# Attention and a two-layer network on one core: the second layer of the first two blocks as seven half-size products, with sums of its weights by VectorE

## The chip, the core and the metric

The kernel runs on one core of a Trainium2 chip. The core has TensorE (PE: matrix products, reading SBUF and writing PSUM), VectorE (DVE), ScalarE (ACT), GpSimd (POOL) and SyncE (SP), each with an instruction stream of its own that runs strictly in order. Engines wait for each other by semaphores. Transfers are issued from a queue of SP, ACT or POOL and moved by 16 shared DMA engines. The metric is the device time of one execution in microseconds (us); lower is better. "PE" is TensorE's row of matmuls and "PEld" its row of weight loads in the profile.

## The reference

```python
# q, k, v: (8, 8, 576, 64) float32; w_in: (512, 2048); w_out: (2048, 512); tau = 0.02
scores = (q @ k.transpose(0, 1, 3, 2)) / sqrt(64)
thresh = scores.max(-1, keepdims=True) - tau
scores = where(scores >= thresh, scores, -1e9)
attn = exp(scores - scores.max(-1, keepdims=True))
attn = attn / (attn.sum(-1, keepdims=True) + 1e-9)
x = (attn @ v).transpose(0, 2, 1, 3).reshape(4608, 512)
h = x @ w_in
out = (h * (1 / (1 + exp(-1.702 * h)))) @ w_out
```

Everything is float32: 64 heads of attention with a threshold one tau below the row's maximum, then a two-layer network over 4608 rows.

## The kernel before

**Units.** Attention is worked in 32 pairs of heads, n = 0 to 31; four pairs make the 576 rows of one batch. The network is worked in 18 blocks of 256 rows. A block can start when the pairs that cover its rows are placed: blocks 0 and 1 need pairs 0 to 3, blocks 2 and 3 need up to pair 7, blocks 4 and 5 up to pair 11.

**A pair.** PE makes transposed scores (L590), ACT copies them out of PSUM (`keep`, L607), VectorE takes maxima (`in_groups`, L613), ACT and VectorE join them across partitions, and the row of maxima is spread over all partitions. VectorE subtracts it (`sub`, L687), ACT masks (L694) and exponentiates (L698), VectorE sums (L613 again), PE multiplies with v (`values`, L709), and VectorE multiplies by the reciprocals of the sums and places the pair into x (`place_x`, L813). From pair 7 on PE interleaves the values of one pair with the scores of the next, tile by tile, because both use the same score tiles.

**Rows.** For pairs 1 and 3 to 6 the row of maxima goes to DRAM (`row_out`, L663) and comes back broadcast (`row_in`, L672); some tiles get it by an accumulating transfer (`add_row`, L678). For pairs 4 to 31 the reciprocals of the sums make the same trip (`sums_out` L778, `sums_in` L785). Each was two transfers, one for each half of the partitions or each head. Pairs below 8 issue them from POOL's queue, the others from SP's.

**The network.** The weights come in 32 pieces (16 of w_in, 16 of w_out) that ACT and VectorE round in a few instructions each (L520, L524, L538, L545). Blocks 0 and 1 run together and plainly: layer one by `mm1_ahead` and `mm1_0` (L876, L887) with 16 chunks of 128 hidden units, `tanh` on ACT and `gelu_0` on VectorE into `g0`, then layer two by `mm2` (L856): 4 row tiles x 16 chunks, 64 matmuls of 512 columns, copied out by ACT (`half`, L863) and stored. From block 2 on both layers use the seven-product scheme on 2x2 quarters: layer one in `product1`, `product0`, `product4` (L955, L1097), layer two in `product` (L1397), in the order P1, P2, P6, P7, P4, P5, P3, each product being 8 matmuls of 256 columns. Its right operands are quarters of w_out and four sums of them (t1, t2, t4 and t3, which is made in place); its left operands are quarters of the activations and their sums on VectorE (`s_sums`, `s_minus`, `s_last`, L1013 to L1024). `read` (L1412, L1419) adds each product into the output quarters. The four sums of w_out are made by `t_minus` (ACT, L997, two sign copies each) and `t_plus` (an accumulating transfer of 1 MB on POOL's queue, L1001), the sums of w_in in the same way by `w_copy` (L922) and `w_plus` (L926). The last four blocks use the scheme twice over (L1248, L1357).

**The order.** Nothing is scheduled at run time. `task` describes each piece of work (engine, estimated cost, rank, predecessors, pools taken and given), and `run_in_order` plays the tasks through a list scheduler with these estimates; whenever an engine is free, the ready task of lowest rank is emitted. FIRST (-9) goes ahead of everything; attention has its pair's number plus a bias by function from the tables EARLY, SECOND and LATER; weights have W_RANK and CV, loads L_RANK; network products have LAST (1000). So on PE attention goes ahead of the network whenever it is ready. A pair n may not start scores before task 16 x (n - LEAD) of the network. Pools bound what is ahead: 3 double banks of PSUM for attention (psA), 2 banks for the network (psM), 6 buffers of x (xT).

**Fillers.** `stay_warm` emits WARM small matmuls on ones at the lowest rank of all, for the time before the network starts (L1463).

## Time and profile before

| | us |
|---|---|
| median of 3 runs | 1224.17 (1223.91 to 1225.14) |
| profiled execution | 1225.39 |
| its span | 1223.6 |
| PE busy | 1212.8 (99% of the span) |
| VectorE busy | 1059.3 (87%) |
| ACT busy | 803.1 (66%) |
| POOL busy | 71.0 (6%) |

The profile is of one execution. Its page gives busy times by engine, the span in 40 slices, the chain of work that ended last, and the costliest groups. Other views of the same trace are quoted too: a table of stretches (columns: the stretch, its length, then busy time and count of PE, PEld, DVE, ACT and POOL, TensorE's granted clock as a share of full speed, the busy share of the DMA engines, GB/s), a timeline (start, length, engine, line, operation, output and inputs, count; in square brackets the idle time before it and what ended it), groups by line and shape (count | busy us, mean ns | idle us before, what ended it), and the instructions of one tile (duration min/median/max in ns, first and last start). A float32 matmul leaves two records that overlap.

### The profile page before, as it was taken

The page shows a single profiled execution, that of the slowest core. Times are in us where ns is not written, and L with a number is a line of the kernel's source. Part 1 is how long each engine was busy: PE and PEld are TensorE (multiplying, and loading weights), DVE is VectorE, ACT ScalarE, POOL GpSimd, SP SyncE. Part 2 cuts the span into 40 slices and gives each one's busy share as a digit, 9 for nine tenths or more (in the row PEclk, how much of TensorE's full clock was granted, in tenths as well). Part 3 has the DMA queues.
Part 4 walks back from the last instruction along what each step waited for, and adds up shares of the span by engine and source line. Part 5 has one row for each costly group of instructions (what it writes and reads, how often), then busy time and mean ns, then how long its engine had stood idle before and what let it go on. Part 6 is the DMA issues. An engine that isn't in the chain of part 4 may idle for free.

```text
span 1223.6 us, 26039 instructions
## 1 busy us (share of the span) xinstructions
PE 1212.8 (99%) x10592; PEld 987.0 (81%) x10592; DVE 1059.3 (87%) x1649; ACT 803.1 (66%) x1203; POOL 71.0 (6%) x115
## 2 busy tenths in 40 slices
...
GB/s 203 252 108 199 196 146 190 209 100 58 101 49 110 49 116 56 75 77 126 101 66 103 71 128 76 65 65 128 91 50 67 101 125 50 129 130 141 141 134 103
DMA packets 202232, 137.12 MB, mean 112 GB/s; under 512 B 146880, under 2 KB 164416, under 8 KB 201984
## 3 DMA queue, kind: packets, MB, share of 16 engines
q1 hardware_dynamic: 189712, 110.21, 33.5%
...
q8 instruction: 83, 1.36, 0.5%
q10 hardware_dynamic: 688, 0.30, 0.1%
q14 instruction: 37, 0.30, 0.1%
HBM read 103.28 MB, written 23.75 MB: 104 GB/s over the span
## 4 chain that ended last, share of the span: by engine, by line
PE 92%; ACT 4%; DMA 2%; DVE 1%; issue 0%; SPq 0%; POOL 0%; POOLq 0%
PE ops L1397 24%; PE pv L709 10%; PE ps L590 10%; PE hps L955 7%; PE hps L1097 7%; PE ps L955 5%; PE ps L1097 5%; PE ops L856 5%; PE hps L887 4%; PE ops L1357 4%; PE hps L1248 4%; PE ps L1357 3%; PE ps L1248 3%; ACT arena L694 1%; ACT arena L698 1%; ACT arena L607 1%
## 5 line engine op out<-in xcount | busy, mean ns | idle before, releaser
L613 DVE TRANSPOSE_TENSOR_REDUCE part<-arena 128x36 f32<-128x1152 f32 (+1 forms) x300 | 363.8, 1239 | 65.9 <-ACT arena L607 49.0
L607 ACT COPY arena<-ps 128x576 f32<-128x576 f32 x288 | 170.5, 644 | 96.8 <-PE ps L590 96.8
L694 ACT ACTIVATE arena<-arena 128x1152 f32<-128x1152 f32 (+1 forms) x160 | 165.1, 1060 | 67.7 <-DVE arena L687 67.5
L687 DVE TENSOR_TENSOR arena<-arena 128x1152 f32<-128x1152 f32 (+1 forms) x150 | 180.9, 1240 | 3.4 <-DMA arena<-row 2.8
L698 ACT ACTIVATE arena<-arena,shift 128x1152 f32<-128x1152 f32 (+1 forms) x160 | 180.5, 1154 | 1.5
L590 PE MATMUL ps<-arena 64*64 64x288 f32 x2304 | 171.4, 408 | 3.4 <-ACT arena L607 3.1
L1397 PE MATMUL ops<-w_out,arena 128*128 128x256 f32 x768 | 174.4, 381 | 0.0
L1397 PEld LDWEIGHTS ops<-w_out,arena 128*128 128x128 f32 x768 | 144.3, 190 | 24.9 <-issue 5.3
L709 PE MATMUL pv<-arena 64*64 64x288 f32 x2176 | 158.5, 405 | 0.0
L590 PEld LDWEIGHTS ps<-arena 64*64 64x64 f32 x2304 | 82.2, 132 | 64.1 <-ACT arena L607 25.3
L709 PEld LDWEIGHTS pv<-arena 64*64 64x64 f32 x2176 | 82.2, 133 | 52.2 <-issue 9.1
L1397 PE MATMUL ops<-arena 128*128 128x256 f32 x528 | 118.1, 379 | 0.0
L1397 PEld LDWEIGHTS ops<-arena 128*128 128x128 f32 x528 | 100.2, 190 | 14.0 <-issue 0.4
L1262 ACT COPY arena<-hps 128x512 f32<-128x512 f32 x44 | 25.7, 584 | 58.4 <-PE hps L1248 58.3
...
L856 PE MATMUL ops<-w_out,arena 128*128 128x512 f32 x128 | 55.9, 595 | 0.0
...
L887 PE MATMUL hps<-xT,w_in 128*128 128x256 f32 x232 | 50.8, 380 | 0.0
L887 PEld LDWEIGHTS hps<-xT,w_in 128*128 128x128 f32 x232 | 43.9, 190 | 6.8 <-issue 0.4
L856 PEld LDWEIGHTS ops<-w_out,arena 128*128 128x128 f32 x128 | 24.1, 190 | 30.1 <-issue 29.5
L955 PEld LDWEIGHTS hps<-xT,w_in 128*128 128x128 f32 x384 | 44.2, 192 | 1.1 <-issue 0.9
L955 PE MATMUL hps<-xT,w_in 128*128 128x128 f32 x384 | 44.9, 275 | 0.0
...
## 6 DMA issues: line engine op xcount, KB each, us to landing
arena<-in_v_dram SPq DMA_DIRECT2D x128, 144.0 KB
...
arena<-in_k_dram SPq DMA_DIRECT2D x112, 72.0 KB
arena<-in_q_dram SPq DMA_DIRECT2D x112, 72.0 KB
...
```

The costliest lines, as they stand in the source:

```text
L590: nc.tensor.matmul(ps[ts(c, KT), h, 0:SH], lhsT=mats[n, 1][ts(h, D), ts(j, KT)], rhs=mats[n, 0][ts(h, D), ts(c, SH)], start=True, stop=True,)
L607: nc.scalar.copy(out=sT[n, t][:, u], in_=pss.pop((n, j))[:, :, 0:SH])
L613: nc.vector.tensor_reduce(out=stats[n, op][:, t * 2 * QB : min(2 * t + 2, NK) * QB], in_=sT[n, t].rearrange("p u h (g d) -> p (u h g) d", ...
L687: engine.tensor_tensor(out=s, in0=s, in1=mbs[n].unsqueeze(1).to_broadcast(list(s.shape)), op=ALU.add if n in BY_DMA else ALU.subtract,)
L694: nc.scalar.activation(out=s, in_=s, func=AF.Prelu, alpha=STEEP)
L698: nc.scalar.activation(out=s, in_=s, func=AF.Exp, scale=SCALE, bias=shift)
L709: nc.tensor.matmul(o[c][ts(h, D), 0:SH], lhsT=left(j, h)[ts(c, KT)], rhs=sT[n, t][ts(c, KT), u, h, :], start=(j == 0), stop=(j == NK - 1),)
L856: nc.tensor.matmul(acc[i], lhsT=g0[:, j, ts(i, P)], rhs=w_out[:, j, :], start=(j == 0), stop=(j == NFC - 1),)
L887: nc.tensor.matmul(hidden[j][:, ts(i, BLK)], lhsT=w_in[:, c, ts(j, P)], rhs=xTs[i][:, c, :], start=(c == 0), stop=(c == NDC - 1), skip_gro ...
L955: nc.tensor.matmul(o[:, ts(j, HT)], lhsT=left[:, c, ts(4 * y + j, P)], rhs=right[:, c, :], start=(x in (P1, P2, P5) and j + c == 0), stop= ...
L1097: nc.tensor.matmul(o[:, ts(j, BLK)], lhsT=left[:, c, ts(j, P)], rhs=right[:, c, :], start=(x in (P1, P2, P5) and j + c == 0), stop=(j + c ...
L1397: nc.tensor.matmul(banks[blk][k][:, ts(o, HM)], lhsT=left[:, j, :], rhs=right[:, j, :], start=(j == 0), stop=(j == HF - 1),)
```

## The change

The second layer of blocks 0 and 1 no longer uses `mm2`. It goes through the seven products of the later blocks, block 0 first, then block 1 (MIXED = 1), 15 tasks each, on the quarters of `g0`. Extra room is found in place: block 0's sums go to the tile that held the tanh values (`th`, kept until P5), to the quarter a11 after P1 has read it (`s_second`), and to a12; block 1's go to block 0's quarters after block 0 is done.

The sums of w_out that these two blocks need are made by `t_whole`, whole subtractions on VectorE, in the order t1, t2, t3, t4_0, as soon as all of w_out is rounded. t4 has a seat of its own for these blocks (t4_0, in the area of score tiles, free once pair 5 is placed); the t4 of the later blocks is made after block 1 in the old way, on ACT and POOL. The last sum of w_in uses the same area and now waits for the end of block 1.

Rows: `row_out`, `row_in` and `sums_in` are one transfer each; `sums_out` still is two, with another layout in DRAM. LEAD is 8 instead of 6. `stay_warm` uses 128 columns and both halves of the partitions, 40 times. The planner's estimates for rows change, and all tables of ranks are replaced.

```diff
     EARLY = {
-        "add_row": 53.65,
...
+        "add_row": 61.4,
...
     SECOND = {
...
     LATER = {
...
     CV = {
...
     def row_out(n):
-        rows[n] = dram.tile([2, S], FP32, name="row", tag="row", bufs=2)
-        for c in range(2):
-            row_queue(n).dma_start(
-                out=rows[n][c : c + 1].rearrange("o (g i) -> (o g) i", i=32),
-                in_=flat[1][ds(c * KT, QB)],
-            )
+        r = dram.tile([P, 32], FP32, name="row", tag="row", bufs=2)
+        row_queue(n).dma_start(out=r, in_=flat[1])
+        rows[n] = r.rearrange("(c g) i -> c (g i)", c=2)[:, 0:S]
     def row_in(n):
...
         row = rows[n]
-        for c in range(2):
-            row_queue(n).dma_start(out=mb[ts(c, KT)], in_=row[c : c + 1].to_broadcast([KT, S]))
+        row_queue(n).dma_start(
+            out=mb,
+            in_=row.unsqueeze(1).to_broadcast([2, KT, S]),
+        )
         mbs[n] = mb
...
             row_queue(n).dma_start(
-                out=rcs[n][c].rearrange("h (g i) -> (h g) i", i=32), in_=flat_s[1][ds(c * KT, QB)]
+                out=rcs[n][:, c].rearrange("h (g i) -> h g i", i=32), in_=flat_s[1][ds(c * KT, QB)]
             )
...
         rc, row = seat(rc_pool(n)), rcs.pop(n)
-        for h in range(2):
-            row_queue(n).dma_start(
-                out=rc[ts(h, D)].rearrange("p (c s) -> p c s", c=2),
-                in_=row[:, h].unsqueeze(0).to_broadcast([D, 2, SH]),
-            )
+        row_queue(n).dma_start(
+            out=rc, in_=row.rearrange("h c s -> h (c s)").unsqueeze(1).to_broadcast([2, D, S])
+        )
         rcs[n] = rc
...
-    g0 = arena[:, ds(2 * HF * HM, 2 * NFC * BLK)].rearrange("p (j t) -> p j t", t=2 * BLK)
     PLAIN = 2
...
     t3 = qb[0][1]
-    T_SUMS = [(t1, t3, qb[0][0]), (t2, qb[1][1], t1), (t4, qb[1][0], t2), (t3, qb[1][1], t3)]
+    g0 = arena[:, ds(2 * HF * HM, 2 * NFC * BLK)].rearrange("p (j t) -> p j t", t=2 * BLK)
+    MIXED = 1
+    qas0 = [
+        [[g0[:, ts(f, HF), ds(x * BLK + h * HT, HT)] for f in range(2)] for h in range(2)]
+        for x in range(2)
+    ]
+    t4_0 = arena2[:, ds(room["s_m1"][0][0] + 2 * HF * HM, HF * HM)].rearrange("p (j m) -> p j m", m=HM)
+    s_0 = [g0[:, HF:NFC, ts(x, HT)] for x in range(2)]
+
+    T_SUMS = [
+        (t1, t3, qb[0][0]), (t2, qb[1][1], t1), (t4_0, qb[1][0], t2), (t3, qb[1][1], t3),
+        (t4, qb[1][0], t2),
+    ]
+
+    def left_sums(blk):
+        if blk == 0:
+            return places["th"].rearrange("p (j t) -> p j t", t=HT), qas0[0][0][0], qas0[0][0][1]
+        return (s_0 if blk == MIXED else sg) + [None]
     def t_minus(x, k):
...
         nc.scalar.activation(out=o, in_=b, func=AF.Copy, scale=-1.0)
+    def t_whole(x, k):
+        o, a, b = (y[:, ts(k, HF // 2), :] for y in T_SUMS[x])
+        nc.vector.tensor_tensor(out=o, in0=a, in1=b, op=ALU.subtract)
+
     def t_plus(x):
...
     def quarters(blk):
+        if blk <= MIXED:
+            return qas0[blk]
         if blk < TAIL:
...
         qa = quarters(blk)
-        a11, a21, a22, u1, u2 = (y[:, ts(k, 4), :] for y in (qa[0][0], qa[1][0], qa[1][1], s1, s2))
+        a11, a21, a22, u1, u2 = (
+            y[:, ts(k, 4), :] for y in (qa[0][0], qa[1][0], qa[1][1], *left_sums(blk)[0:2])
+        )
         nc.vector.tensor_tensor(out=u1, in0=a21, in1=a22, op=ALU.add)
+        if blk == 0:
+            return
         nc.vector.tensor_tensor(out=u2, in0=u1, in1=a11, op=ALU.subtract)
...
         nc.vector.tensor_tensor(out=a21, in0=a11, in1=a21, op=ALU.subtract)
+    def s_second(k):
+        u1, a11 = (y[:, ts(k, 4), :] for y in left_sums(0)[0:2])
+        nc.vector.tensor_tensor(out=a11, in0=u1, in1=a11, op=ALU.subtract)
+
     def s_last(blk, k):
-        a12, u = (y[:, ts(k, 4), :] for y in (quarters(blk)[0][1], s2))
-        nc.vector.tensor_tensor(out=u, in0=a12, in1=u, op=ALU.subtract)
+        a12, u = (y[:, ts(k, 4), :] for y in (quarters(blk)[0][1], left_sums(blk)[1]))
+        nc.vector.tensor_tensor(out=u if blk else a12, in0=a12, in1=u, op=ALU.subtract)
     P1, P2, P6, P7, P4, P5, P3 = range(7)
...
         left, right, k, o = PRODUCTS[x]
+        if blk <= MIXED and x in (P6, P5, P3):
+            left = left_sums(blk)[{P5: 0, P6: 1, P3: 1 if blk else 2}[x]]
+        if blk <= MIXED and x == P4:
+            right = t4_0
         if isinstance(left, tuple):
...
         d = psM.tile([P, BANK], FP32, name="up", tag="mo")
-        for _ in range(2):
-            nc.tensor.matmul(d[0:D, 0:D], lhsT=ones[0:KT], rhs=ones[0:KT], start=True, stop=True)
+        for r in range(2):
+            nc.tensor.matmul(
+                d[ts(r, KT), 0:P], lhsT=ones[ts(r, KT)], rhs=eye[ts(r, KT)], start=True, stop=True
+            )
     def tau_terms():
...
     SUMS_BY_DMA = range(4, NP)
-    LEAD = 6
+    LEAD = 8
     ROWS_BY_POOL = range(8)
...
     T_RANK = FIRST
-    W_RANK = (76.72, 196.12, 138.01, 508.95, -9.25, -19.99)
+    W_RANK = (31.97, 148.79, 230.02, 650.9, -20.74, 160.11)
     W_TIME = 1.8
-    WARM = 44
+    WARM = 40
     ROUND_BY_ACT = range(0)
...
     early_mm1, held_sums = [], []
+
+    late_seat = []
     def first_blocks():
...
             gelus[j] = task("DVE", 0.59, FIRST, gelu_0, j, after=[a],
-                give=("psM", "io") + (("xT",) if j == NFC - 1 else ()),
+                give=("psM", "io"),
             )
         plain1[:] = ffn[-1:]
-        for i in range(PLAIN * BLK // P):
-            for p in range(NFC // 2):
-                after = ffn[-1:] + [gelus[2 * p], gelus[2 * p + 1]]
-                after += ready_w[n_in + 2 * p : n_in + 2 * p + 2]
-                ffn.append(task(
-                    "PE", FFU, LAST, mm2, i, p, after=after, take=("psM",) if p == 0 else (),
-                ))
-                last_mm2[p // 2 % 2] = ffn[-1]
-            a = task("ACT", 0.5, FIRST, half, i, after=ffn[-1:], take=("osb",), give=("psM",))
-            task("SP", 0.6, FIRST, store_0, i, after=[a], give=("osb",), lag=2.2)
-
-
-        for x in range(4):
-            after = t_ready[-1:] + (ffn[-1:] if x > 1 else []) + ready_w[n_in:]
+        def t_sum(x, behind):
+            after = t_ready[-1:] + behind + ready_w[n_in:]
+            if x < 4:
+                for k in range(2):
+                    after = [task("DVE", 1.33, T_RANK, t_whole, x, k, after=after)]
+                t_ready.extend(after)
+                return
             for k in range(2):
...
             t_ready.append(transfer("DMW", 6.5, a, 1, lag=2.0))
+        for x in (0, 1, 3, 2):
+            t_sum(x, [])
+        late_seat.extend(y for y in range(len(tasks)) if tasks[y][3] is t_whole and tasks[y][4][0] == 2)
+        all_gelus = [gelus[j] for j in range(NFC)]
+        sums = [task("DVE", 0.66, FIRST, s_sums, 0, y, after=all_gelus) for y in range(2)]
+        minus = [task("DVE", 0.6, FIRST, s_minus, 0, y, after=[sums[y]]) for y in range(2)]
+        second(0, {x: [all_gelus, []] for x in (P1, P2, P4)}, sums, minus)
+        sums = [task("DVE", 1.33, FIRST, s_sums, MIXED, y, after=ffn[-1:]) for y in range(2)]
+        minus = [task("DVE", 0.6, FIRST, s_minus, MIXED, y, after=[sums[y]]) for y in range(2)]
+        second(MIXED, {x: [[], []] for x in (P1, P2, P4)}, sums, minus)
+        t_sum(4, ffn[-1:])
+
     def w_sums():
...
             after = w_done[-1:] if w_done else [placed[SINGLE - 2]] + ready_w[:n_in]
-            if x == 2:
-                after = after + plain1
+            if x >= 2:
+                after = after + (plain1 if x == 2 else ffn[-1:])
             a = [task("ACT", 0.95, T_RANK, w_copy, x, c, after=after) for c in range(2)]
...
     last5, seated = [], []
-    T_OF = {P6: 2, P7: 4, P4: 3, P5: 1}
+    T_OF = {P6: 2, P7: 3, P4: 5, P5: 1}
     def second(blk, ready, sums, minus):
...
             if x in T_OF:
-                after += t_ready[: T_OF[x]]
+                after += t_ready[: T_OF[x] - (blk <= MIXED and x == P4)]
+            if blk == 0 and x in (P1, P2):
+                after += ready_w[n_in + HF * (x == P2) + js[0] : n_in + HF * (x == P2) + js[1]]
             if x in ready:
...
             else:
-                after.append((minus if x == P7 else sums)[y])
+                after.append((minus if x == P7 else sums2 if blk == 0 and x == P6 else sums)[y])
             after += [reads[z] for z in range(x) if PRODUCTS[z][2] == PRODUCTS[x][2]]
...
                 take=("psM",) if x in (P1, P2) and p == 0 else (),
+                give=("xT",) if blk == 0 and x == P5 and p else (),
             ))
+            if blk == 0 and x == P1 and p == 3:
+                sums2 = [
+                    task("DVE", 0.66, FIRST, s_second, k, after=ffn[-1:] + sums + minus) for k in range(2)
+                ]
             last_mm2[y] = ffn[-1]
...
         )
+        if n == SINGLE - 2:
+            for x in late_seat:
+                tasks[x][5].append(placed[n])
         while hp == NPAIR - 1 and (next_blk + 1) * BLK <= (b + 1) * S:
...
     crossed = {"max": [], "sums": []}
-    L_RANK = (3.45, -109.6, -17.9, 36.14, 35.53, 42.62, 27.86, 146.49, 9.14, 81.46, 255.02, -17.35, -3.34, -15.75, -2.02, -2.69, 30.05, -3.25, -48.27, 6.8, -9.58, 10.21, 37.91, -22.41)
+    L_RANK = (-273.04, -257.76, 475.26, -9.28, -177.25, 91.89, -5.96, 31.25, 19.51, 13.32, 33.9, 75.09, 8.15, 4.01, 61.18, 35.61, -3.35, -20.55, 21.32, 16.46, -6.76, 63.98, 0.15, 28.84)
     def load_rank(n, which):
...
         slow = 1.1 if n < 2 * NPAIR else 1.0
-        rq = ("POOL", 1.4, "DMW", 2.2) if n in ROWS_BY_POOL else ("SP", 1.0, "DMS", 1.7)
-        flow = 2.9 if n in (0, 1, 4) else 0.0
+        rq = ("POOL", 1.4, "DMW", 1.0) if n in ROWS_BY_POOL else ("SP", 1.0, "DMS", 1.7)
+        flow = 2.9 if n in (0, 1, 4, 5) else 1.5
         by_sp = n not in ROWS_BY_POOL
...
                 a = task(
-                    "PE", 0.26, LAST + 1.0, stay_warm, x, after=warmth[:1] + [pq, pk],
+                    "PE", 0.24, LAST + 1.0, stay_warm, x, after=warmth[:1] + [pq, pk],
                     take=("psM",), give=("psM",),
...
             a = task("DVE", 0.22, r, turn_rows, n, after=[a])
-            a = transfer(rq[2], 0.3 + 0.4 * by_sp, task(rq[0], 0.65 * rq[1], r, row_out, n, after=[a]), lag=1.7 - 0.4 * by_sp + flow)
-            spread[n] = task(rq[0], 1.1 * rq[1], r, row_in, n, after=[a], take=own(n, "mb"))
+            a = transfer(rq[2], 0.3 + 0.4 * by_sp, task(rq[0], 0.42 * rq[1], r, row_out, n, after=[a]), lag=1.3 + flow)
+            spread[n] = task(rq[0], 0.5 * rq[1], r, row_in, n, after=[a], take=own(n, "mb"))
             m = transfer(rq[2], 1.1, spread[n], 0 if by_sp else 1, give=() if n in ADDED else ("row",), lag=rq[3] + flow)
...
                 a = transfer(rq[2], 0.3 + 0.4 * by_sp, task(rq[0], 0.65 * rq[1], r, sums_out, n, after=[a]), lag=1.7 - 0.4 * by_sp)
-                a = task(rq[0], 1.2 * rq[1], r, sums_in, n, after=[a] + (second_rc if n == SECOND_RC else []), take=(rc_pool(n),))
+                a = task(rq[0], 0.5 * rq[1], r, sums_in, n, after=[a] + (second_rc if n == SECOND_RC else []), take=(rc_pool(n),))
                 summed[n] = transfer(rq[2], 1.1, a, 0 if by_sp else 1, give=("row_s",), lag=rq[3])
...
```

152 lines of the change are left out of this document (76 added, 76 removed).

## The prediction

> **What bounds the kernel now.** I read the page first (busy times, then the 40 slices), then the busy time by stretches of 50 us, then the timelines of PE, VectorE and GpSimd around the part that the change rewrites. The profiled execution took 1225.39 us with a span of 1223.6; the 1.79 us around the span are not touched. It lies 1.22 us above the median of 1224.17, so I work out differences and take them from the median.
>
> ```profile
> PE 1212.8 (99%) x10592; PEld 987.0 (81%) x10592; DVE 1059.3 (87%) x1649; ACT 803.1 (66%) x1203; POOL 71.0 (6%) x115
> ```
>
> PE is busy in 99% of the span, so time goes where PE's instructions go. But PE's list contains fillers and waits early on, as the stretches show (columns: PE, weight loads, DVE, ACT, POOL, granted clock, DMA share, GB/s):
>
> ```profile
> 50.00:100.00 50.00, 46.41 (x670) 28.85 (x666) 44.79 (x78) 49.52 (x70) 10.25 (x16) 1.00 0.62 134
> 100.00:150.00 50.00, 49.86 (x353) 39.57 (x350) 49.49 (x72) 49.78 (x76) 9.87 (x14) 1.00 0.75 202
> 150.00:200.00 50.00, 50.00 (x332) 30.23 (x334) 34.11 (x55) 39.37 (x55) 14.46 (x18) 1.00 0.82 163
> 200.00:250.00 50.00, 50.00 (x301) 27.45 (x295) 33.33 (x47) 30.35 (x45) 7.64 (x9) 1.00 0.89 201
> 1050.00:1100.00 50.00, 49.59 (x445) 49.43 (x444) 48.55 (x96) 23.34 (x43) 0.00 (x0) 1.00 0.44 132
> 1200.00:1223.60 23.60, 20.43 (x183) 20.24 (x181) 16.52 (x49) 0.28 (x1) 0.00 (x0) 1.00 0.30 93
> ```
>
> Until about 100 us ACT is full (49.52 of 50) and PE waits for it; from there to the last slice PE has next to no gap. The changed products lie at 164 to 242, where PE is full and VectorE is idle for a third of the time. What PE runs there can only be shortened if the next thing on PE is ready sooner too. That next thing is the first product of layer one of block 2 (L955), which needs the attention pairs 4 to 7:
>
> ```profile
> 164.46 1.88 PE L856 MATMUL ops<-w_out,arena 128*128 128x512 f32 x4
> 229.19 1.15 PE L590 MATMUL ps<-arena 64*64 64x288 f32 x16
> 242.39 3.73 PE L955 MATMUL hps<-xT,w_in 128*128 128x128 f32 x32
> 245.96 3.74 PE L955 MATMUL ps<-xT,w_in 128*128 128x128 f32 x32
> 377.60 3.73 PE L955 MATMUL hps<-xT,w_in 128*128 128x128 f32 x32
> ```
> ```profile
> 208.89 0.95 DVE L813 TENSOR_TENSOR xT<-pv,arena 128x192 f32<-128x192 f32 x4 [4.43 <-DMA arena<-row_s]
> 242.66 0.95 DVE L813 TENSOR_TENSOR xT<-pv,arena 128x192 f32<-128x192 f32 x4 [2.46 <-DMA arena<-row_s]
> 376.95 0.91 DVE L813 TENSOR_TENSOR xT<-pv,arena 128x128 f32<-128x128 f32 x4
> ```
>
> L813 places an attention pair into x. Pair 7 is placed at 242.66 to 243.61. The first product (242.39) reads pairs 4 and 5 only; the second (245.96) reads 6 and 7. So the slack at block 2 is 245.96 - 243.61 = 2.35 us, and at block 4, where pair 11 is the last, 377.60 + 3.57 - 377.86 = 3.3 us. This slack, not PE's sum alone, decides what the change is worth.
>
> **The change, part by part.** *Products.* Removed: 64 matmuls of 512 columns. Added: 7 products for each of 2 blocks, 8 matmuls of 256 columns each, 112 in all. Both prices are in the trace (each matmul has two records):
>
> ```profile
> 164.62:242.55 77.93, 55.74 (x128) 23.72 (x127) 1.00 0.90 188
> 278.44:299.36 20.92, 20.92 (x96) 18.09 (x96) 1.00 0.28 58
> ```
>
> The first row is L856 alone, 55.74 us; the second a stretch of nothing but L1397, 20.92 / 48 = 0.436 us a matmul. 112 x 0.436 = 48.8, so PE's list gets shorter by **6.9 us**.
>
> *Sums on VectorE.* Four sums of w_out quarters in two halves each, 128x1024; no row has that form. Bounds are 1.20 us (the 128x1152 row times 1024/1152) and 1.38 (two of the 128x512 row); I take 1.2, since its row is the nearest in width: 8 x 1.2 = 9.6. The sums of activations: 8 of 128x512 for each block, 16 x 0.69 = 11.0. Readings of the products into the output: 7 for each block, 14 x 0.41 = 5.7. Together **26.3 us** more of VectorE. ACT loses six sign copies at 1.05 (6.3 us) and four copies of 0.60, and gains two of 0.38.
>
> ```profile
> L687 DVE TENSOR_TENSOR arena<-arena 128x1152 f32<-128x1152 f32 x123 | 162.2, 1348 | 3.4 <-DMA arena<-row 2.8
> L1014 DVE TENSOR_TENSOR arena<-arena 128x512 f32<-128x512 f32 x18 | 12.5, 692 | 0.6
> L613 DVE TRANSPOSE_TENSOR_REDUCE part<-arena 128x36 f32<-128x1152 f32 x240 | 321.9, 1362 | 63.9 <-ACT arena L607 48.7 <-ACT arena L698 14.1
> L1419 DVE SCALAR_TENSOR_TENSOR osb<-ops,osb 128x256 f32<-128x256 f32 x84 | 33.5, 410 | 9.0 <-PE ops L1397 8.2 <-issue 0.6
> L997 ACT ACTIVATE arena<-arena 128x1024 f32<-128x1024 f32 x4 | 4.0, 1049 | 0.0
> L863 ACT ACTIVATE osb<-ops 128x512 f32<-128x512 f32 x4 | 2.4, 597 | 5.2 <-PE ops L856 5.2
> L1412 ACT ACTIVATE osb<-ops 128x256 f32<-128x256 f32 x12 | 4.5, 379 | 7.9 <-PE ops L1397 7.9
> 165.90:242.50 76.60, 76.60 (x488) 36.88 (x486) 44.81 (x61) 49.66 (x69) 20.47 (x26) 1.00 0.92 192
> ```
>
> In the stretch of the last row VectorE has 76.6 - 44.8 = 31.8 us free, and the stretch itself is to shrink to 69.7. 44.8 + 26.3 = 71.1: a little more than fits. Some 7.5 us of it are pair 8's maxima (four of 1.36 and smaller ones), which block 2 does not wait for, so what must be done before it is some 63 of 69.7. The cover is there, but thin.
>
> *Does P6 wait for the w_out sums?* The last piece of w_out is finished at 170.56 by the row below; two sums in two halves each are 4.8 us, so the second sum is there at 175.4. PE is through layer one at 164.46 and then has P1 and P2 (16 x 0.436 = 7.0) and the 4.6 us of pair 5's values: 176.0. I take no wait; without pair 5 in that gap it is 175.4 - 171.4 = 4 us, the upper bound. P7 and P4 follow 3.5 us apart, the sums 2.4 apart, so they don't wait if P6 doesn't. P4's sum also needs pair 5 placed (175.90 now, its VectorE queue then holding the other sums), P4 itself starts at 183: nothing.
>
> ```profile
> 169.87 0.69 DVE L545 SCALAR_TENSOR_TENSOR w_out<-arena,w_out 128x512 int32<-128x512 int32 x1 [1.09 <-ACT w_out L524]
> 166.27 4.59 PE L709 MATMUL pv<-arena 64*64 64x288 f32 x72
> ```
>
> *The attention chain up to pair 7.* It gains where rows travel by GpSimd's queue:
>
> ```profile
> 193.21 1.13 POOL L778 DMA_DIRECT2D row_s<-flat_s  x2 [2.33 <-DVE flat_s L773]
> 197.93 0.92 POOL L926 DMA_DIRECT2D arena<-arena  x1 [3.59 <-ACT arena L922]
> 200.64 1.26 POOL L785 DMA_DIRECT2D arena<-row_s  x2 [1.79 <-issue]
> 222.48 1.19 POOL L926 DMA_DIRECT2D arena<-w_in  x1 [12.37 <-ACT arena L922]
> 229.19 1.11 POOL L778 DMA_DIRECT2D row_s<-flat_s  x2 [5.53 <-DVE flat_s L773]
> 235.53 1.23 POOL L785 DMA_DIRECT2D arena<-row_s  x2 [5.23 <-DMA row_s<-flat_s]
> ```
>
> Pair 6's row of sums left at 193.21, its return was queued behind a w_in sum (L926) that itself waited for ACT, and VectorE then stood for 4.43 us until 208.89, with pair 7's subtractions behind it. Pair 7's return stood for 5.23 us because its first leg shared the queue with the 1 MB sum issued at 222.48. The w_out sums that blocks 0 and 1 need leave this queue, the w_in sum issued at 222.48 moves behind block 1, and the return is one issue instead of two (0.6 us each). So at most 4.43 + 5.23 = 9.7 us come back, and at least nothing, if another w_in sum stands in the way again. Against that stand some 20 us of new VectorE work at the highest rank before pair 7; the idle time that it falls into is partly the chain's own waiting, so between 0 and 20 - (69.7 - 63) = 13 us are lost. I take two thirds of the gain (the 5.23 with the sum at 222.48 gone, and little of the 4.43, as the one at 197.93 stays) and a third of the loss, 6.5 - 4 = **2.5 us earlier**. Then PE needs the second product of block 2 at 245.96 - 6.9 = 239.1, pair 7 is there at 241.1, and PE waits 2.0 us: **6.9 - 2.0 = 4.9 us gained**. With no movement of the chain it would be 2.35, with 9.7 the whole 6.9; with 13 lost, PE would lose 10.6.
>
> *The wider bound* (8 instead of 6 pairs ahead): pair 8's scores run at 229.19, while the old bound releases them with the first matmuls of the removed products at 164.46, 65 us before. It does not bind there: 0, with at most the slack of 2.35 to 3.3 gained later.
>
> *One transfer per row on SP* (pair 8 on): off PE's path; 0 either way, bounds -1 to +1 (one issue of 0.6 saved, a larger packet in its place).
>
> *Fillers for PE's clock* (40 of 0.24 instead of 44 of 0.26, wider, on both halves of the rows):
>
> ```profile
> 36.00:38.00 2.00, 0.83 (x11) 0.59 (x11) 2.00 (x3) 1.97 (x3) 2.00 (x4) 0.94 1.02 320
> 38.00:40.00 2.00, 2.00 (x38) 2.00 (x42) 0.50 (x2) 1.97 (x3) 1.41 (x2) 0.50 1.04 336
> 40.00:42.00 2.00, 2.00 (x29) 2.00 (x26) 1.88 (x4) 1.97 (x3) 0.00 (x0) 0.71 1.04 267
> L1463 PE MATMUL up<-ones 64*64 64x64 f32 x176 | 13.1, 222 | 0.2
> L524 ACT ACTIVATE w_in<-w_in,rebias 128x512 int32<-128x512 f32 x16 | 11.5, 734 | 0.0
> 20.00:104.00 84.00, 78.20 (x1152) 56.04 (x1149) 76.38 (x122) 82.39 (x117) 17.87 (x24) 0.98 0.79 183
> ```
>
> The granted clock falls to 0.50 and 0.71 right behind a run of fillers, which costs PE 2 x 0.5 + 2 x 0.29 = 1.6 us. But ACT, busy 82.39 of 84 us up to 104, sets the end of this part: 0, bounds 0 and -1.6. The Trainium skill ("TensorE: Matmul & The Clock Gate", Part 1) has the clock halve after an idle window of some 3.4 us; the row has no such gap (1.17 us idle), so here the trace differs, and by the page wider fillers would be worth nothing. The sum is the same by both.
>
> *New ranks.* They reorder everything, the part before 104 us most. PE idles 84 - 78.2 = 5.8 us there and fills 13.1, so 18.9 is the most that a better order could give; but ACT has 1.6 us free, so more than that needs weight conversions moved behind the start of layer one. The same rows allow a loss: each piece of w_in that is converted before pair 3 instead of after it puts two ACT instructions of 0.7 us (L524 and its like) into the way. I take 0, bounds -8 and +8 (six pieces of 1.4). In the tail VectorE is at 48.55 of 50 with PE idle 0.41 us: ranks there can cost some us, hardly give any.
>
> **Sum:** -6.9 + 2.0 + 0 = -4.9, 1224.17 - 4.9 = **1219.3 us**.
>
> **Rivals.** *(a) The head gets shorter too.* For it: 18.9 us of idle and filler; against it: ACT is full. With five us from there and the row's full gain: 1224.17 - 6.9 - 5 = 1212.3. *(b) The attention chain takes it all.* Pair 7 comes 2.4 us later than now; PE's wait is 6.9 and the time stays, 1224. For it: VectorE's 71.1 us in a stretch of 69.7. *(c) VectorE becomes the bound from 100 to 240* and pair 7 slips by two thirds of the 13 us, 8.7; PE then waits 8.7 + 6.9 - 2.35 = 13.3 in place of the 6.9 saved: 1230.5, slower. It is slower from the point where pair 7 slips by more than 2.35. For it: 49.49 of 50 us of VectorE before the stretch already. Against: GpSimd's queue holds pair 7 up by 9.7 us now. *(d) The ranks lengthen the head* by some 10 us, against a gain of 5: 1229. *(e) The products don't get cheaper*, as PE's own sums of columns fall but each product pays an entry: the 0.436 above has the entries in it, so I give it nothing.
>
> A rule that speaks against sums on VectorE: the Trainium skill ("SBUF — State Buffer", SBUF: two separate sides) says that a VectorE operation with two SBUF inputs and a GpSimd one that reads SBUF lock each other out. In the trace GpSimd's issues don't stretch beside such operations, so it changes only the chance of (b) a little:
>
> ```profile
> L663 POOL DMA_DIRECT2D row<-flat x10: 523/546/560, 26.5 to 168.0; - x10
> ```
>
> **How the numbers follow.** Forecast (1216 to 1221.5) 0.40, (a) 0.22, (b) 0.11, (c) 0.17, (d) 0.10. Faster, by over 0.2% or 2.4 us, about what measurement tells from nothing: 0.62; same 0.11; slower 0.27. The range leaves out the better end of (a) and the worse ends of (c) and (d): 1208 to 1231.5; the forecast's own is 1216 to 1221.5.
>
> **What would show it.** Seven groups of L1397-like products of 3.5 us for each of blocks 0 and 1 where L856 was, 48.8 us in sum. Pair 7's placing at some 240 us with little waiting on row_s. A PE wait of about 2 us ahead of block 2's second product. VectorE above 90% from 165 to 236. The start of unbroken PE work still near 104. Wrong would make it: that start moved by several us; or PE gaps after 240 that before did not have; or P6 waiting for VectorE.

## The result, and the profile after

The changed kernel takes **1347.81 us** (median of 6 runs, 1343.06 to 1353.64) against 1224.92 us for the kernel before on the same chip: a ratio of 1.1002, 95% interval 1.0966 to 1.1038. That is 122.9 us slower, where 4.9 us faster was forecast and 1231.5 us was the upper end of the range.

The page of the changed kernel's profiled execution (1353.64 us, span 1351.9), busy times and the slices for TensorE:

```profile
span 1351.9 us, 26195 instructions
PE 1245.5 (92%) x10672; PEld 1014.8 (75%) x10672; DVE 1082.6 (80%) x1687; ACT 795.5 (59%) x1193; POOL 62.0 (5%) x98
...
PE   8598778879989999999999999999999999899999
...
PEclk9898889999989999999999999999999999999999
```

Before, PE had 10.8 us without work (1223.6 - 1212.8); now it has 106.4, and though its list is shorter it is busy 32.7 us longer, since part of the work ran at a lower clock (the mean granted clock is 0.964, before 0.999). The holes are not at the changed products alone: they begin at 50 us and go on to the end. The stretches (columns as in the prediction):

```profile
50.00:100.00 50.00, 37.09 (x494) 20.47 (x486) 33.43 (x57) 37.70 (x54) 5.16 (x6) 0.86 0.46 97
...
150.00:200.00 50.00, 34.85 (x244) 26.27 (x245) 30.99 (x46) 34.59 (x49) 6.29 (x8) 0.84 0.45 105
...
500.00:550.00 50.00, 44.35 (x384) 37.45 (x383) 39.80 (x55) 33.13 (x43) 0.00 (x0) 0.99 0.27 74
...
1150.00:1200.00 50.00, 45.55 (x374) 41.69 (x373) 41.62 (x78) 22.75 (x32) 0.00 (x0) 0.97 0.33 91
```

No engine is full in them, ACT and VectorE neither, so this is waiting and not work. The groups by line say for what; first the placing of a pair in the kernel before, then the placing and the subtraction of the maxima in the changed kernel:

```profile
L813 DVE TENSOR_TENSOR xT<-pv,arena 128x256 f32<-128x256 f32 (+7 forms) x128 | 29.8, 293 | 10.3 <-DMA arena<-row_s 9.5 <-DVE arena L796 0.5
```
```profile
L810 DVE TENSOR_TENSOR xT<-pv,arena 128x256 f32<-128x256 f32 (+7 forms) x128 | 30.2, 297 | 107.3 <-DMA arena<-row_s 107.0 <-PE pv L708 0.2
L686 DVE TENSOR_TENSOR arena<-arena 128x1152 f32<-128x1152 f32 (+1 forms) x150 | 180.7, 1241 | 25.9 <-DMA arena<-row 25.1
```

VectorE stands 107.0 us for returning rows of sums (9.5 before) and 25.1 us for returning rows of maxima (2.8 before). Everything behind it in its list stands too. One such place on the timeline of the changed kernel, and what the DMA engines did meanwhile (stretches of 2 us):

```profile
162.55 1.36 DVE L686 TENSOR_TENSOR arena<-arena 128x1152 f32<-128x1152 f32 x1 [7.68 <-DMA arena<-row]
...
164.56 11.61 PE L883 MATMUL hps<-xT,w_in 128*128 128x256 f32 x40 [6.82 <-DVE arena L889]
```
```profile
160.00:162.00 2.00, 0.00 (x0) 0.00 (x0) 0.00 (x0) 0.85 (x2) 0.00 (x0) 0.50 0.14 50
162.00:164.00 2.00, 0.00 (x0) 0.00 (x0) 1.45 (x2) 0.06 (x1) 0.00 (x0) 0.50 0.15 27
164.00:166.00 2.00, 1.44 (x4) 1.17 (x4) 2.00 (x3) 1.10 (x1) 0.00 (x0) 0.50 0.15 26
```

VectorE waits 7.68 us for a row, PE behind it 6.82, and the DMA engines are all but idle: a busy share of 0.14 to 0.15, little above two of sixteen (0.125), at 26 to 50 GB/s. So the row isn't queued behind other transfers; it is slow itself. And the granted clock is 0.50, which PE pays for after the wait too. The same in one return from SP's queue, before and after:

```profile
572.82 1.36 SPq L785 DMA_DIRECT2D arena<-row_s  x2
577.26 0.95 DVE L813 TENSOR_TENSOR xT<-pv,arena 128x256 f32<-128x256 f32 x4 [2.58 <-DMA arena<-row_s]
```
```profile
1073.08 0.52 SPq L783 DMA_DIRECT2D arena<-row_s  x1
1082.16 0.95 DVE L810 TENSOR_TENSOR xT<-pv,arena 128x64 f32<-128x64 f32 x4 [4.19 <-DMA arena<-row_s]
```

From the issue to the placing that waits for it: 4.44 us before, 9.08 after.

### The profile page after: what moved, and what is told of

Same layout as the page of the kernel before. It is cut to its first block, busy times and chain, and to the rows that moved or that the text cites. A ratio compares the mean times of both kernels' runs of the same rounds, so it can differ in the third digit from the quotient of the medians.

```text
span 1351.9 us, 26195 instructions
## 1 busy us (share of the span) xinstructions
PE 1245.5 (92%) x10672; PEld 1014.8 (75%) x10672; DVE 1082.6 (80%) x1687; ACT 795.5 (59%) x1193; POOL 62.0 (5%) x98
## 5 line engine op out<-in xcount | busy, mean ns | idle before, releaser
L613 DVE TRANSPOSE_TENSOR_REDUCE part<-arena 128x36 f32<-128x1152 f32 x300 | 363.0, 1237 | 39.2 <-ACT arena L607 34.2
L1428 PE MATMUL ops<-w_out,arena 128*128 128x256 f32 x896 | 205.4, 383 | 8.3 <-DVE osb L1450 8.3
L686 DVE TENSOR_TENSOR arena<-arena 128x1152 f32<-128x1152 f32 (+1 forms) x150 | 180.7, 1241 | 25.9 <-DMA arena<-row 25.1
L590 PE MATMUL ps<-arena 64*64 64x288 f32 x2304 | 175.3, 415 | 12.5 <-ACT arena L607 8.3
L1428 PE MATMUL ops<-arena 128*128 128x256 f32 x576 | 129.3, 380 | 1.7 <-DVE osb L1450 1.5
L1428 PEld LDWEIGHTS ops<-arena 128*128 128x128 f32 x576 | 109.2, 190 | 17.8 <-DVE osb L1450 2.1
L810 DVE TENSOR_TENSOR xT<-pv,arena 128x256 f32<-128x256 f32 (+7 forms) x128 | 30.2, 297 | 107.3 <-DMA arena<-row_s 107.0
L883 PE MATMUL hps<-xT,w_in 128*128 128x256 f32 x232 | 58.1, 412 | 16.9 <-DVE arena L889 16.9
L883 PEld LDWEIGHTS hps<-xT,w_in 128*128 128x128 f32 x232 | 47.2, 207 | 28.0 <-DVE arena L889 19.6
L951 PE MATMUL hps<-xT,w_in 128*128 128x128 f32 x384 | 51.1, 294 | 17.2 <-DVE osb L1450 16.9
L951 PEld LDWEIGHTS hps<-xT,w_in 128*128 128x128 f32 x384 | 49.1, 208 | 19.3 <-DVE osb L1450 18.2
L1124 PE MATMUL hps<-xT,w_in 128*128 128x256 f32 x192 | 45.6, 390 | 5.8 <-DVE osb L1450 5.8
```

Of the source, the lines that this page charges most:

```text
L590: nc.tensor.matmul(ps[ts(c, KT), h, 0:SH], lhsT=mats[n, 1][ts(h, D), ts(j, KT)], rhs=mats[n, 0][ts(h, D), ts(c, SH)], start=True, stop=True,)
L613: nc.vector.tensor_reduce(out=stats[n, op][:, t * 2 * QB : min(2 * t + 2, NK) * QB], in_=sT[n, t].rearrange("p u h (g d) -> p (u h g) d", ...
L686: engine.tensor_tensor(out=s, in0=s, in1=mbs[n].unsqueeze(1).to_broadcast(list(s.shape)), op=ALU.add if n in BY_DMA else ALU.subtract,)
L883: nc.tensor.matmul(hidden[j][:, ts(i, BLK)], lhsT=w_in[:, c, ts(j, P)], rhs=xTs[i][:, c, :], start=(c == 0), stop=(c == NDC - 1), skip_gro ...
L951: nc.tensor.matmul(o[:, ts(j, HT)], lhsT=left[:, c, ts(4 * y + j, P)], rhs=right[:, c, :], start=(x in (P1, P2, P5) and j + c == 0), stop= ...
L1428: nc.tensor.matmul(banks[blk][k][:, ts(o, HM)], lhsT=left[:, j, :], rhs=right[:, j, :], start=(j == 0), stop=(j == HF - 1),)
```

## Theories

**T1**: the new return has a source of 2 x 64 x 576 elements, two rows, each read 64 times. The transfer is shared out by that outermost dimension, so 288 KB go over 2 of 16 engines and land 4 to 5 us later; the order written in advance puts the placing where VectorE stands then. Before, each of two transfers had 64 in front. The Trainium skill says so ("DMA: Bandwidth & Descriptors", Why a DMA increments its semaphore by 16 and not by 1): the number of engines is the largest up to 16 that divides the slowest dimension of both sides, here 2. I had not weighed it; the DMA share of 0.15 above agrees. **T2**: the new ranks and the order that follows from them do the harm, and the rows only show it. **T3**: VectorE is the bound with its new sums, rival (c) of the prediction. **T4**: one transfer in place of two is slow in itself, whatever its shape.

## The experiments

**1. The returns in two again.** The changed kernel; only the way back of both rows is as two transfers of 64 partitions:

```diff
     def row_in(n):
-        row_queue(n).dma_start(
-            out=mb,
-            in_=row.unsqueeze(1).to_broadcast([2, KT, S]),
-        )
+        for c in range(2):
+            row_queue(n).dma_start(out=mb[ts(c, KT)], in_=row[c : c + 1].to_broadcast([KT, S]))
...
     def sums_in(n):
-        row_queue(n).dma_start(
-            out=rc, in_=row.rearrange("h c s -> h (c s)").unsqueeze(1).to_broadcast([2, D, S])
-        )
+        for h in range(2):
+            row_queue(n).dma_start(
+                out=rc[ts(h, D)], in_=row.rearrange("h c s -> h (c s)")[h : h + 1].to_broadcast([D, S])
+            )
```

> The changed kernel, with each return of a row (maxima: row_in, reciprocals of sums: sums_in) as two transfers of 64 partitions each instead of one whose source has an outermost dimension of 2; order of all other instructions, ranks, products and sums as in the changed kernel. T1 (the single transfer, split by its dimension of 2, goes over 2 of the 16 DMA engines and lands about 4 us later): the placings' wait for row_s falls from 107.0 us to under 25, PE idle from 106 to under 25 us, time 1212 to 1240. T2 (new ranks and order do the harm): 1330 to 1350, waits elsewhere. T3 (VectorE is the bound since it makes the sums): 1320 or more. T4 (a single transfer is slow in itself, over however many engines): as T1 here.

Measured: **1233.95 us** (1232.74 to 1237.59), a ratio to before of 1.0073 (1.0054 to 1.0092). 113.9 of the 122.9 us are gone. The placings, by line:

```profile
L809 DVE TENSOR_TENSOR xT<-pv,arena 128x256 f32<-128x256 f32 (+7 forms) x128 | 29.9, 293 | 15.9 <-DMA arena<-row_s 15.7 <-PE pv L706 0.2
```

The wait fell from 107.0 to 15.7. PE's idle time is 23.1 us (span 1235.8, busy 1212.7). T2 and T3 are out as the main cause.

**2. All four row functions as before**, so the way out too:

```diff
     def row_out(n):
-        r = dram.tile([P, 32], FP32, name="row", tag="row", bufs=2)
-        row_queue(n).dma_start(out=r, in_=flat[1])
-        rows[n] = r.rearrange("(c g) i -> c (g i)", c=2)[:, 0:S]
+        rows[n] = dram.tile([2, S], FP32, name="row", tag="row", bufs=2)
+        for c in range(2):
+            row_queue(n).dma_start(
+                out=rows[n][c : c + 1].rearrange("o (g i) -> (o g) i", i=32),
+                in_=flat[1][ds(c * KT, QB)],
+            )
...
-                out=rcs[n][:, c].rearrange("h (g i) -> h g i", i=32), in_=flat_s[1][ds(c * KT, QB)]
+                out=rcs[n][c].rearrange("h (g i) -> (h g) i", i=32), in_=flat_s[1][ds(c * KT, QB)]
```

> The changed kernel with all four row functions in the form of the kernel before (two transfers out, two back, for both rows); ranks, bound, products and sums as changed. T1 and T4: within 6 us of the run with only the returns in two, so 1212 to 1240; T2 and T3: 1320 to 1350. My prediction without its row term says 1219.

Measured: **1231.66 us** (1230.74 to 1231.9), ratio 1.0048 (1.0033 to 1.0063). By the medians the way out is worth 2.3 us (the runs of experiment 1 spread from 1232.74 to 1237.59), the way back the rest of 116.2. But 6 us above before and 12 above my forecast remain: the rows are not the whole story (experiments 6 to 10).

**3. The row functions alone, in the kernel before**: the four functions in the changed form (the diff of 1 and 2 the other way round), nothing else.

> The kernel before with only the four row functions in the changed form; ranks, fillers, layer two of blocks 0 and 1 as before. T1 and T4: each of the 28 returns lands some 4 us later, and where the written order leaves no room PE waits: 1260 to 1345, and most of the 124 us that the change cost. T2 and T3: 1223 to 1230, nothing.

Measured: **1327.26 us** (1326.01 to 1331.65), ratio 1.0836 (1.0811 to 1.0862). With the old ranks and without a single new sum the old kernel loses 102 us by the four functions. Its placings wait as in the changed kernel:

```profile
L810 DVE TENSOR_TENSOR xT<-pv,arena 128x256 f32<-128x256 f32 (+7 forms) x128 | 30.4, 298 | 96.5 <-DMA arena<-row_s 95.8
```

**4. The forms by themselves**, on a chip that does nothing else:

```diff
+    def two_64(queue, t):
+        for c in range(2):
+            queue.dma_start(out=t[ds(c * 64, 64)], in_=rows[c : c + 1].to_broadcast([64, S]))
+    def one_2x64(queue, t):
+        queue.dma_start(out=t, in_=rows[0:2].unsqueeze(1).to_broadcast([2, 64, S]))
+    def one_16x8(queue, t):
+        queue.dma_start(out=t, in_=rows[0:16].unsqueeze(1).to_broadcast([16, 8, S]))
+    def two_62(queue, t):
+        for c in range(2):
+            queue.dma_start(out=t[ds(c * 64, 62)], in_=rows[c : c + 1].to_broadcast([62, S]))
...
+        for _ in range(6):
+            form(queue, t)
+            nc.vector.tensor_tensor(out=small, in0=small, in1=t[:, 0:32], op=ALU.add)
```

> No part of the reference is computed: only the transfers of rows, alone on an idle chip, each form six times, each followed by one small VectorE addition that waits for it; the wait is the price. Forms: two transfers of 64 partitions (two64, and halves64 with two pieces per partition), one with an outermost dimension of 2 (one2x64), one of the same size with an outermost dimension of 16 (one16x8), one of 128 partitions from one row (one128), two of 62 partitions (two62); three of them on GpSimd's queue too; and three forms of the way out. T1: one2x64 8 to 14 us against 4 to 5 for two64, one16x8 and one128 as quick as two64 (within 0.7 us), two62 slow like one2x64 though it is two transfers. T4: one16x8 and one128 are as slow as one2x64, two62 is as quick as two64. T2 and T3: all forms within 1 us.

The names in the profile are cut before digits. The idle time before VectorE's addition is the sum of five waits (the first transfer of a form was already under way). First the groups; then, for the two forms that share a name, the timeline (two_64 at 36.38, two_62 at 147.83); then the stretches in which only one_2x64 and only one_16x8 ran (columns: VectorE, POOL, clock, DMA share, GB/s):

```profile
L63 DVE TENSOR_TENSOR small<-small,halves 128x32 f32<-128x32 f32 x6 | 1.2, 192 | 19.2 <-DMA halves<-in_q_dram 19.1
L63 DVE TENSOR_TENSOR small<-small,one2x 128x32 f32<-128x32 f32 x6 | 1.2, 192 | 41.0 <-DMA one2x<-in_q_dram 41.0
L63 DVE TENSOR_TENSOR small<-small,one16x 128x32 f32<-128x32 f32 x6 | 1.2, 192 | 17.4 <-DMA one16x<-in_q_dram 17.4
L63 DVE TENSOR_TENSOR small<-small,one 128x32 f32<-128x32 f32 x6 | 1.2, 192 | 16.3 <-DMA one<-in_q_dram 16.3
```
```profile
36.38 0.19 DVE L63 TENSOR_TENSOR small<-small,two 128x32 f32<-128x32 f32 x1 [3.56 <-DMA two<-in_q_dram]
...
147.83 0.19 DVE L63 TENSOR_TENSOR small<-small,two 128x32 f32<-128x32 f32 x1 [8.47 <-DMA two<-in_q_dram]
```
```profile
61.20:103.00 41.80, 0.85 (x5) 0.00 (x0) 1.00 0.09 35
103.30:121.60 18.30, 0.92 (x6) 0.00 (x0) 1.00 0.25 81
```

One transfer of 2 x 64 rows takes 41.0 / 5 = 8.2 us. One of 16 x 8 takes 3.5, one of 128 times one row 3.3, the old forms 3.6 to 3.9 (without the first two waits of the program, 14.73 and 6.41). On GpSimd's queue it is the same: 8.6 for 2 x 64, 3.6 for 16 x 8, 3.9 for two of 64. Two transfers of 62 partitions take 8.5, though they are two and carry less: 62 can be divided by 2 and not by 4, 8 or 16. So neither the number of transfers nor the bytes count, but the divisor of the outermost dimension. One transfer of 128 or 16 x 8 is even the quickest. I had expected 4 to 5 us for the old form, so it was quicker than I thought. Three forms of the way out ran too, but overlapped each other, so no price comes out of them.

**5. The same inside the kernel.** The changed kernel with one transfer per return; each half of a row stands in DRAM eight times, so that the outermost dimension is 16:

```diff
-            in_=row.unsqueeze(1).to_broadcast([2, KT, S]),
+            in_=row.rearrange("c r s -> (c r) s").unsqueeze(1).to_broadcast([16, 8, S]),
...
-            out=rc, in_=row.rearrange("h c s -> h (c s)").unsqueeze(1).to_broadcast([2, D, S])
+            out=rc,
+            in_=row.rearrange("h r c s -> (h r) (c s)").unsqueeze(1).to_broadcast([16, 8, S]),
```

> The changed kernel, its returns still one transfer each and its order unchanged, but each half of the row stands eight times in DRAM (the way out writes the copies, in two and four transfers), so that the outermost dimension of the return's source is 16 instead of 2. T1 (what costs is the number of engines that the dimension allows): the placings' wait for row_s falls from 107.0 us to under 30, time 1228 to 1245. T4 (one transfer in place of two is slow inside this kernel, though not alone): 1330 to 1350.

Measured: **1238.72 us** (1236.46 to 1239.34), ratio 1.0102 (1.0085 to 1.012). The placings wait 17.2 us:

```profile
L815 DVE TENSOR_TENSOR xT<-pv,arena 128x256 f32<-128x256 f32 (+7 forms) x128 | 29.9, 293 | 17.4 <-DMA arena<-row_s 17.2 <-PE pv L711 0.2
```

T4 is out and T1 holds in the kernel too. It is 7 us above experiment 2. The dearer way out (copies, up to four issues) is the likely reason, but I did not take that apart.

**6. What is left: the new order alone.** The kernel before, its plain layer two and its rows, with the changed ranks, bound, fillers and estimates:

```diff
     EARLY = {
-        "add_row": 53.65,
+        "add_row": 61.4,
...
-    LEAD = 6
+    LEAD = 8
...
-        rq = ("POOL", 1.4, "DMW", 2.2) if n in ROWS_BY_POOL else ("SP", 1.0, "DMS", 1.7)
+        rq = ("POOL", 1.4, "DMW", 1.0) if n in ROWS_BY_POOL else ("SP", 1.0, "DMS", 1.7)
...
```

> The kernel before (layer two of blocks 0 and 1 by 64 matmuls of 512 columns, rows in two transfers each) with the changed kernel's ranks, wider bound, fillers and estimates for rows, and nothing else. If the new order itself makes the head longer (as in the run with rows as before, where layer one's long run on TensorE starts at 112.1 instead of 105.8): that start moves to 110 to 114 and the time is 1229 to 1236, the products having saved some 1 us there. If the late head comes from the sums of w_out or from anything else in the products: start at 104 to 107, time 1222 to 1228. My prediction's term for ranks and bound was 0.

Measured: **1236.11 us** (1235.13 to 1239.06), ratio 1.0098 (1.0079 to 1.0117): the order alone costs 12 us (9.7 to 14.3). Ranks, bound, fillers and the planner's estimates for rows were changed together here, so their shares stay open. The time lies just above the range that I had given, and the products' gain is larger than the 1 us that I had expected. PE's timeline, first of the kernel before, then of this run and of experiment 2, shows layer one's long run and block 2's first product (242.39 before):

```profile
105.84 32.11 PE L887 MATMUL hps<-xT,w_in 128*128 128x256 f32 x148
```
```profile
109.90 28.09 PE L887 MATMUL hps<-xT,w_in 128*128 128x256 f32 x128 [1.21 <-DVE arena L893]
...
252.39 3.73 PE L955 MATMUL hps<-xT,w_in 128*128 128x128 f32 x32
```
```profile
112.10 28.12 PE L886 MATMUL hps<-xT,w_in 128*128 128x256 f32 x128 [1.19 <-DVE arena L892]
...
184.75 3.69 PE L1431 MATMUL ops<-arena 128*128 128x256 f32 x16 [1.26 <-issue]
...
223.59 3.72 PE L1431 MATMUL ops<-w_out,arena 128*128 128x256 f32 x16 [1.43 <-DVE osb L1453]
228.93 3.72 PE L1431 MATMUL ops<-arena,arena 128*128 128x256 f32 x16 [1.62 <-DVE osb L1453]
...
248.50 3.88 PE L954 MATMUL hps<-xT,w_in 128*128 128x128 f32 x32
```

Both start layer one late (4.1 and 6.3 us). A likely cause is seen at the first row that travels, pair 1's: GpSimd sends its maxima out at 26.54 in the kernel before and at 34.76 in experiment 2 (34.98 here). In experiment 10, whose order starts layer one at 106.91, they leave at 27.57. The lines are of the kernel before, experiment 2, experiment 10, and twice of experiment 2:

```profile
26.54 1.05 POOL L663 DMA_DIRECT2D row<-flat  x2 [24.20 <-DVE flat L647]
```
```profile
34.76 1.33 POOL L663 DMA_DIRECT2D row<-flat  x2 [32.42 <-DVE flat L647]
```
```profile
27.57 1.05 POOL L663 DMA_DIRECT2D row<-flat  x2 [25.23 <-DVE flat L647]
```
```profile
51.62 3.90 DVE L687 TENSOR_TENSOR arena<-arena 128x1152 f32<-128x1152 f32 x3 [4.97 <-DMA arena<-row]
```
```profile
52.00:54.00 2.00, 0.00 (x0) 0.00 (x0) 2.00 (x2) 0.99 (x1) 0.00 (x0) 0.92 1.21 213
54.00:56.00 2.00, 0.09 (x4) 0.09 (x8) 2.00 (x3) 2.00 (x4) 0.00 (x0) 0.50 1.16 219
56.00:58.00 2.00, 2.00 (x20) 1.07 (x24) 1.97 (x7) 1.94 (x5) 0.00 (x0) 0.50 1.10 254
```

In experiment 2 VectorE stands 4.97 us for that row, PE has next to nothing from 52 to 56, and the clock then is at 0.50. The DMA engines are full at that time, but they were full on this row's way in the kernel before too (shares of 1.02 and 1.04 from 36 to 42, in the prediction), so what is new is that it leaves 8.2 us later. That is rival (d) of the prediction in place and kind. Which rank puts pair 1 behind was not taken apart. It is not all that the order costs either: in the run with the ranks alone block 2 starts 10.0 us late, and only 4.1 of that stand ahead of layer one. From layer one's long run to block 2's first product it takes 142.49 us against 136.55 before. PE is idle for 4.1 us of it and was never idle there before; the longest wait, 2.94 us, is for ACT's copies of scores.

With the same ranks (the list is played anew, so it is not instruction for instruction the same order), the products bring the time from 1236.11 to 1231.66: **4.5 us** by the medians, 6.1 by the ratios (1.0098 - 1.0048 of 1225), and block 2 starts 3.9 us sooner.

**7. VectorE's load.** Experiment 2 with the activations' sums of blocks 0 and 1 made over 8 of each 128 columns, so most of these sums is left out; the count and order of instructions stay:

```diff
+    def few(blk, y):
+        return y[:, :, 0:8] if blk <= MIXED else y
...
-        a11, a21 = (y[:, ts(k, 4), :] for y in (qa[0][0], qa[1][0]))
+        a11, a21 = (few(blk, y[:, ts(k, 4), :]) for y in (qa[0][0], qa[1][0]))
```

> The changed kernel with rows as before, and the sums of activations of blocks 0 and 1 on VectorE only over 8 of each 128 columns (the rest of these sums is left out; number and order of instructions unchanged): 16 instructions of 0.68 us become about 0.15 us, some 8 us of VectorE less between 180 and 230. If VectorE's load is what holds the seven products up (waits of 1.26, 1.43 and 1.62 us before P6, P7 and P4): these waits go and the time is 3 to 5 us under the run with rows as before (1231.7), so 1226.5 to 1229. If the order or the rows hold them up: 1230 to 1233.

Measured: **1228.13 us** (1226.58 to 1230.72), ratio 1.003 (1.0019 to 1.0042), so 3.5 us less than experiment 2 by the medians, 2.2 by the ratios, whose intervals overlap (1.0033 to 1.0063 there). In the profiled runs, from layer one's long run to block 2's first product, it takes 134.52 us against 136.40. The wait ahead of P6 is gone, but not those of block 1:

```profile
184.10 3.62 PE L1434 MATMUL ops<-arena 128*128 128x256 f32 x16
...
223.82 3.72 PE L1434 MATMUL ops<-w_out,arena 128*128 128x256 f32 x16 [2.13 <-DVE osb L1456]
228.16 3.72 PE L1434 MATMUL ops<-arena,arena 128*128 128x256 f32 x16 [0.62 <-DVE osb L1456]
```

So VectorE's load costs some 2 us here, 3.5 at most, close to what these runs can tell from nothing. The waits at 223.82 and 228.16 are for readings of earlier products. The reading that the second one needs stands behind three subtractions of the next pair in VectorE's list. The reading that the first one needs stands behind a placing that waits for its row, and the maxima that follow it:

```profile
217.05 0.95 DVE L813 TENSOR_TENSOR xT<-pv,arena 128x192 f32<-128x192 f32 x4 [5.07 <-DMA arena<-row_s]
```

Both are a matter of order and of rows, not of the sums' length.

**8. The fillers' width** (64 columns on 64 rows again, in experiment 2):

```diff
-        for r in range(2):
-            nc.tensor.matmul(
-                d[ts(r, KT), 0:P], lhsT=ones[ts(r, KT)], rhs=eye[ts(r, KT)], start=True, stop=True
-            )
+        for _ in range(2):
+            nc.tensor.matmul(d[0:D, 0:D], lhsT=ones[0:KT], rhs=ones[0:KT], start=True, stop=True)
```

> The changed kernel with rows as before, and the fillers 64 columns wide on 64 rows again (as many as in the changed kernel, in the same places). If their width matters for the clock: granted clock of 0.5 behind them again between 36 and 46, and up to 1.6 us longer than the run with rows as before. My term for them was 0: 1231 to 1233.

Measured: **1231.59 us** (1230.96 to 1232.35), the same as experiment 2, and the clock is 1.00 in all stretches from 36 to 50. So the width is worth nothing in this order. Why the clock fell to 0.50 at 38 in the kernel before stays open; this order has real work in that place.

**9. The bound at 6 again**, in experiment 2:

```diff
-    LEAD = 8
+    LEAD = 6
```

> The changed kernel with rows as before and the bound of attention at 6 instead of 8 pairs; ranks as changed, so the list comes out in another order from where the bound binds. If the wider bound is worth nothing (my term): within 2 us of the run with rows as before, 1230 to 1234. If the new ranks live on the wider bound: 1236 or more; if the bound does harm: under 1229.

Measured: **1234.91 us** (1233.47 to 1236.03), ratio 1.0082 (1.0068 to 1.0097), 3.3 us slower than with 8, between the two expectations. The new ranks use the wider bound; the whole list changes with it, so this is no price of the bound by itself.

**10. An order made for rows as they are.** Experiment 2 with the old estimates for rows, and the ranks (and ranks of their own for the new sums) searched anew by the planner's own end time, with 26 fillers:

```diff
-        rq = ("POOL", 1.4, "DMW", 1.0) if n in ROWS_BY_POOL else ("SP", 1.0, "DMS", 1.7)
+        rq = ("POOL", 1.4, "DMW", 2.2) if n in ROWS_BY_POOL else ("SP", 1.0, "DMS", 1.7)
...
-                    after = [task("DVE", 1.33, T_RANK, t_whole, x, k, after=after)]
+                    after = [task("DVE", 1.33, S_RANK[x], t_whole, x, k, after=after)]
...
```

> The changed kernel with rows in two transfers, the estimates for rows of the kernel before, and ranks searched anew for these estimates (bound 8, 26 fillers), nothing else. If the 6.5 us that the run with rows as before stands above the kernel before are a matter of order: 1219 to 1227, layer one's long run starting at 104 to 109, and block 2's first product at 238 to 244. If they belong to the products (VectorE's sums) whatever the order: 1229 to 1235, block 2's first product at 246 or later.

Measured: **1223.83 us** (1221.59 to 1225.51, 11 runs) against 1224.39, a ratio of 0.9991 (0.9983 to 1.0): no difference that counts. Its PE timeline:

```profile
106.91 20.99 PE L886 MATMUL hps<-xT,w_in 128*128 128x256 f32 x96 [1.64 <-DVE arena L892]
...
181.94 1.78 PE L590 MATMUL ps<-arena 64*64 64x288 f32 x16 [2.76 <-ACT arena L607]
...
242.01 3.73 PE L954 MATMUL hps<-xT,w_in 128*128 128x128 f32 x32
```

The products wait for VectorE no more, layer one starts 1.1 us later than before and block 2 0.4 us sooner. So what stood above the kernel before was a matter of order. PE's work between these two points is 5.3 us less than before (131.27 against 136.55), but PE is idle for 3.8 us of that stretch, where it was never idle before, each time ahead of scores that wait for ACT (2.76 at 181.94). That and the later start give back nearly all of the products' gain. A version that clearly beats the kernel before was not found.

## Why the prediction was wrong

The whole, by medians of the runs above:

| part | forecast, us | measured, us | by |
|---|---|---|---|
| rows in one transfer | 0 (-1 to +1) on SP; a gain on GpSimd | +116.2 | changed kernel less experiment 2 |
| ranks, bound, fillers, estimates | 0 (-8 to +8) | +12 (9.7 to 14.3) | experiment 6 |
| products with their sums, net | -4.9 | -4.5 to -6.1 | experiment 2 less 6 |

**The step that failed** is "One transfer per row on SP (pair 8 on): off PE's path; 0 either way, bounds -1 to +1 (one issue of 0.6 saved, a larger packet in its place)". I counted issues and not engines. The return went from 3.6 to 8.2 us alone (experiment 4), from 4.44 to 9.08 on SP's queue in the kernel. "Off PE's path" was wrong in kind as well: VectorE's list is written out in advance with the placing at a fixed place, so a late row stops subtractions, sums and readings behind it, ACT after them and PE at last. The row that should have warned me stood in the prediction: pair 6's placing had waited 4.43 us for a return already. The planner counts half a microsecond of issue, 1.1 of transfer and 1.7 until it is seen, 3.3 in all, for this return; an order written for 3.3 us met 8.2.

**GpSimd's return** as "one issue instead of two (0.6 each)" failed likewise. The issue itself did get shorter, though not by 0.6: of the four in the changed kernel three take 0.81 to 1.05 us and one 2.29, where two together took 1.26 and 1.23 in the rows of the prediction. But the row lands late. Pair 7's took 7.1 us from its issue to the placing that waited for it (235.53 to 242.66), and takes 10.5 in the changed kernel:

```profile
294.09 0.82 POOL L783 DMA_DIRECT2D arena<-row_s  x1 [2.23 <-issue]
304.56 0.95 DVE L810 TENSOR_TENSOR xT<-pv,arena 128x192 f32<-128x192 f32 x4 [7.90 <-DMA arena<-row_s]
```

**New ranks**: taken as 0 with bounds of 8 to each side; 12 lies outside. I had priced what ACT could lose to pieces of w_in, and not that the first pair's row could leave 8 us later and leave VectorE and PE without work, nor new waits for ACT between layer one and block 2. Rival (d) had the place and a size of 10, at a chance of 0.10.

**Products**: the 6.9 us less 2.0 of waiting were forecast as 4.9, and 4.5 to 6.1 came with the changed ranks. The 6.9 is roughly borne out (from layer one's long run to block 2's first product PE is busy 130.85 us in experiment 2 and 138.41 in experiment 6), but that the rest fits is in part luck. The waiting lies elsewhere: not ahead of block 2's second product, but 1.26 ahead of P6 (taken as 0, bound 4) and 1.43 and 1.62 in block 1, where readings stand behind a waiting placing and behind subtractions, which I did not foresee. And in another order (experiment 10) next to nothing of the gain is left.

**VectorE's 26.3 us** right in size: the new sums of w_out in experiment 2 take 1.2 us each as taken (1216 ns, and 1200 to 1217 for the other forms), and nothing of VectorE's went away: its instructions rise by 38, which are the 8 + 16 + 14 new ones. Their own times add up to 26.1 us. Its busy time rises by only 21.1 (1059.3 to 1080.4), because records of instructions that follow each other overlap: two sums of 0.68 take 1.28 together.

```profile
L1017 DVE TENSOR_TENSOR arena<-w_out,arena 128x1024 f32<-128x1024 f32 x4 | 4.7, 1216 | 0.0
```

Rival (c), VectorE as the bound, is not what made the kernel slow; its load costs some 2 us (experiment 7). **Pair 7** was forecast to be placed by 241.1 for an unchanged head; with layer one 6.3 us later that is 247.4, and experiment 2 has it placed by 249.14 (248.19 and 0.95). **Fillers** 0: right as far as their width goes (experiment 8). **The wider bound** 0: with these ranks its removal costs 3.3 us (experiment 9).
